# Mixture of experts on one core: row gathers issued during the second product, the second matrix's blocks taken in the order 0, 2, 1, 3, and the over-capacity path ahead of the last product

## The chip, the core and the metric

The kernel runs on one core of a Trainium2 chip. The core has TensorE (PE in the profile: matrix products; PEld is its weight load), VectorE (DVE), ScalarE (ACT), GpSimd (POOL) and SyncE (SP, which here issues the plain DMAs). GpSimd issues the DMAs that gather and scatter rows by an index. The metric is device microseconds of one execution; lower is better.

## The reference, cut to what matters

Attention over 4 x 576 tokens is followed by a dense block, and then by a mixture of 8 experts. The change lies in the experts alone. Each of the 2304 tokens goes to the one expert with the largest gate logit:

```
logits = x @ w_gate                      # x: 2304 x 512
e_idx = np.argmax(logits, axis=1)
...
for e in range(8):
    mask = e_idx == e
    h = np.maximum(x[mask] @ w1[e], 0.0)     # first product, 512 -> 1024
    ye = h @ w2[e]                           # second product, 1024 -> 512
    out[mask] = gate_w[mask, None] * eom[mask, e, None] * ye
```

## The kernel before

Everything is float32. Each product is made of three passes (`mm3`, `mm3n`): a matrix is split into a rounded part (`hi`) and the remainder (`lo`), and hi·hi, hi·lo and lo·hi are summed in PSUM. In `mm3n` the three passes are lines L425, L426 and L427; in `mm3` L419, L420 and L421. The third pass reads the `lo` part of the weights.

The token rows were written to a table `yd` in DRAM by the dense block. The experts are ranked by their token count and taken in an order `r` = 0 to 7 with fixed capacities `CAPS` = 352, 336, 320, 304, 288, 288, 272, 384, so three blocks of at most 128 rows for each. Per expert:

- `x_gather` (L732, POOL) fetches up to 128 rows per DMA into one of four `xr` buffers; `x_prep` transposes them on PE (L750) and splits them on ACT and DVE (L754).
- `ew_load` (SP, L763 for the first matrix, L766 for the second) brings a quarter of a weight matrix, "block" 0 to 3, 512 KB, into one of four `raw` buffers. It must wait until the split that used the buffer before is done.
- `ew_split` makes `hi` with a cast on ACT (L775) and `lo` with a subtraction (L777): blocks 0 and 2 on POOL, blocks 1 and 3 on DVE. The first matrix's tiles are `W0` to `W3` (hi) and `W4` to `W7` (lo), the second matrix's `W8` to `W11` (hi) and `W12` to `W15` (lo).
- `ga_pair` is a quarter of the first product: two of eight `h` tiles, f = 2i and 2i+1, from block i. ACT and DVE split each result (L803).
- `gb_step` is a quarter (`dc`) of the second product. It runs over f = 0 to 7 and takes block f // 2, so every `gb_step` needs all four blocks of the second matrix. ACT copies its result (L845).
- `o_step` transposes a block of results back (L861), DVE scales it into `orow` (L850) and POOL scatters it into the output (L851).

The instructions of the loop over `r` are issued on each engine exactly in the order of the code (`manual_schedule`), shown below with its main lines. A stage `r` has two halves: four `gb_step`s of expert r, with the first matrix and the rows of expert r+1 prepared in between, then four `ga_pair`s of expert r+1, with its second matrix prepared in between. `by_width` (L654) chooses by a branch on PE how many columns a product runs over. In stage 0, `overflow_tables` (L874) computes on DVE which experts have more tokens than their capacity.

The last expert's second product is `gb_rows`: three blocks of 24 products each, DVE's `orow`, and a scatter. `overflow` (L914) then reads one number into a register on every engine (L915) and branches (L916): if some expert is over its capacity, a loop does the surplus tokens in a general way. With these inputs none is, and the engines jump over the body. On the jump's arm each engine waits until its own earlier instructions have signalled, and adds to its semaphores what the skipped body would have added.

```
            for dc in range(KD):
                gb_step(r, dc)
                ...
                ew_split(r + 1, 0, dc)
                ew_load(r + 1, 1, dc)
            for i in range(4):
                ew_split(r + 1, 1, i)
                if i == 0 and r + 2 < E:
                    x_gather(r + 2)
                ga_pair(r + 1, 2 * i)
                if i < NBLK[r]:
                    o_step(r, i)
```

Of the kernel before, what the change touches and what calls it, by code (L numbers as in the profile page):

```python
# [22 lines left out]
NT, DM, DF, E = 2304, 512, 1024, 8  # L23
# [12 lines left out]
NBLK = [-(-c // P) for c in CAPS]  # L36
NBM = max(NBLK)
CMAX = max(CAPS)
CUTS = (0, 16, 48)
NEG = -1e30  # L40
OOB = 1.0e6
RING = 2 * G
# [7 lines left out]
def attention_moe_kernel(ctx: ExitStack, tc: tile.TileContext, q, k, vw_in, v4_in, w1, w2, w3, w_out,  # L50
# [32 lines left out]
    for j in range(4):  # L83
        nc.gpsimd.iota(ci[32 * j:32 * j + 32, 0:32], pattern=[[1, 32]], base=0, channel_multiplier=-1)
    nc.vector.tensor_copy(cj[:, 0:32], ci[:, 0:32])
    nc.vector.tensor_scalar(cj[:, 32:64], cj[:, 0:32], 0.0, NEG, op0=ALU.is_lt, op1=ALU.mult)
    nc.vector.tensor_scalar(cj[:, 64:96], cj[:, 0:32], 6.0, NEG, op0=ALU.is_gt, op1=ALU.mult)
    nc.vector.tensor_tensor(
        mask, cj[:, 32:64].unsqueeze(1).to_broadcast([P, 6, 32]),
        cj[:, 64:96].unsqueeze(1).to_broadcast([P, 6, 32]), op=ALU.add)  # L90
    nc.vector.memset(mask[0:32, 0, 0:3], NEG)
    nc.vector.memset(mask[96:128, 5, 27:32], NEG)
    eps4 = mt([P, 1], F32, "eps4")
# [551 lines left out]
    def by_width(r, C, products):  # L645
# [3 lines left out]
        def arm(a, b):  # L649
            if b - a == 1:  # L650
                products(C - CUTS[a])
                return
            m = (a + b) // 2
            with tc.If(rt["n"][r] > C - CUTS[m]) as cond:  # L654
                arm(a, m)
            with cond.Else():
                arm(m, b)

        arm(0, len(CUTS))

# [55 lines left out]
        pe[0] = next((i for i in reversed(nc.cur_bb.bb.instructions) if i.engine == mybir.EngineType.PE), None)  # L716
        return res

    def x_gather(r, half=None):
        C = CAPS[r]  # L720
        d = rt.setdefault("xr", {})
        for b in range(NBLK[r]):
            n = min(P, C - P * b)
            if (r, b) not in d:
                d[r, b] = bp.tile([P, DM], F32, name="xr", tag="xr", bufs=4)
            dst, src = d[r, b][0:n], yd
            if half == 0:
                dst, src = dst[:, 0:DM // 2], yd.rearrange("n (t d) -> (n t) d", t=2)
            elif half == 1:
                dst, src = dst[:, DM // 2:DM], yh  # L730
            idx = rt["g2"][0:n, b:b + 1] if half == 0 else rt["gi"][0:n, r, b:b + 1]
            ins = nc.gpsimd.indirect_dma_start(out=dst, out_offset=None, in_=src,  # L732
                                               in_offset=bass.IndirectOffsetOnAxis(ap=idx, axis=0))
        return ins
# [23 lines left out]
    def ew_load(r, m, i, t=None):  # L758
        reg = reg_of(r)
        if t is None:  # L760
            t = bp.tile([P, 1024], F32, name="raw", tag="raw", bufs=4)
        if m == 0:
            ins = nc.sync.dma_start(out=t,  # L763
                              in_=e_w1[bass.ds(reg, 1), P * i:P * i + P, :].rearrange("o p n -> p (o n)"))
        else:
            ins = nc.sync.dma_start(out=t,  # L766
                              in_=e_w2[bass.ds(reg, 1), P * i:P * i + P, :].rearrange("o p n -> p (o n)"))
        raws[r, m, i] = t
        return ins

    def ew_split(r, m, i):
        t = raws.pop((r, m, i))
        hi = w_tile(8 * m + i, [P, 1024])
        lo = w_tile(8 * m + 4 + i, [P, 1024])
        nc.scalar.copy(out=hi, in_=t)  # L775
        eng = nc.vector if i % 2 != (r == 0 and m == 1) or (r == 0 and m == 0) else nc.gpsimd
        ins = eng.tensor_tensor(lo, t, hi.bitcast(F32), op=ALU.subtract)  # L777
        ew[r, m, i] = (hi, lo)
        return ins
# [94 lines left out]
    def overflow_tables():  # L874
        cnt, rank = rt["cnt"], rt["rank"]
        s3 = [P, E, E]
        s4 = [P, E, NC]
        cap_t = bt([P, E], "cap_t")
        for r in range(E):
            nc.vector.memset(cap_t[:, r:r + 1], float(RANK_CAPS[r]))  # L880
        cm = bt(s3, "cm")
        nc.vector.tensor_tensor(cm, bc(rank, s3, 2), bc(i8, s3, 1), op=ALU.is_equal)
        nc.vector.tensor_tensor(cm, cm, bc(cap_t, s3, 1), op=ALU.mult)
        cap = bt([P, E], "cap")
        nc.vector.tensor_reduce(out=cap, in_=cm, axis=AX.X, op=ALU.add)
        ov = bt([P, E], "ov")
        nc.vector.tensor_tensor(ov, cnt, cap, op=ALU.is_gt)
        b0 = bt([P, NC], "b0")
        nc.vector.tensor_scalar(b0, i18, float(P), None, op0=ALU.mult)
        f1 = bt(s4, "f1")  # L890
        f2 = bt(s4, "f2")
        nc.vector.tensor_tensor(f1, bc(cnt, s4, 2), bc(b0, s4, 1), op=ALU.is_gt)
        nc.vector.tensor_scalar(b0, b0, float(P), None, op0=ALU.add)
        nc.vector.tensor_tensor(f2, bc(b0, s4, 1), bc(cap, s4, 2), op=ALU.is_gt)
        nc.vector.tensor_tensor(f1, f1, f2, op=ALU.mult)
        nc.vector.tensor_tensor(f1, f1, bc(ov, s4, 2), op=ALU.mult)
        fi = bt([P, E * NC], "fi", I32)
        nc.vector.tensor_copy(fi, f1.rearrange("p e b -> p (e b)"))
        an = bt([P, 1], "an")
        nc.vector.tensor_reduce(out=an, in_=ov, axis=AX.X, op=ALU.add)  # L900
        ai = bt([P, 1], "ai", I32)
        nc.vector.tensor_copy(ai, an)
        ee = bt([P, E, NC], "ee", I32)
        nc.vector.tensor_copy(ee, bc(i8, s4, 2))
        tt = tab[:, 0]
        gi = bt(s4, "ogi", I32)
        si = bt(s4, "osi", I32)
        nc.vector.tensor_scalar(gi, tt, -1.0, 0.0, op0=ALU.add, op1=ALU.max)
        nc.vector.tensor_scalar(f2, tt, 0.0, OOB, op0=ALU.is_equal, op1=ALU.mult)
        nc.vector.scalar_tensor_tensor(si.rearrange("p e b -> p (e b)"), tt.rearrange("p e b -> p (e b)"), -1.0,  # L910
                                       f2.rearrange("p e b -> p (e b)"), op0=ALU.add, op1=ALU.add)
        rt.update(fi=fi, ai=ai, ee=ee, ogi=gi, osi=si)
# [198 lines left out]
    et = mybir.EngineType  # L1111
    with tc.manual_schedule(engines={et.PE, et.DVE, et.Activation, et.Pool, et.SP}):
        for r in range(E - 1):
            for dc in range(KD):
                gb_step(r, dc)
                if dc < NBLK[r + 1]:
                    x_prep(r + 1, dc)
                ew_split(r + 1, 0, dc)
                ew_load(r + 1, 1, dc)
            for i in range(4):  # L1120
                ew_split(r + 1, 1, i)
                if i == 0 and r + 2 < E:
                    x_gather(r + 2)
                ga_pair(r + 1, 2 * i)
                if i < NBLK[r]:
                    o_step(r, i)
                if r + 2 < E:
                    ew_load(r + 2, 0, i)
                if (r, i) == (0, 1):
                    overflow_tables()  # L1130
        for b in range(NBLK[E - 1]):
            gb_rows(E - 1, b)
    overflow()
    bctx.close()


# [58 lines left out]
```

## Time and profile before

| what | value |
|---|---|
| median of 3 runs | 729.62 us (725.38 to 732.04) |
| the profiled execution's own time | 732.17 us |
| its span, first to last instruction | 730.1 us |
| mean granted TensorE clock | 0.983 |
| PE busy, share of the span | 95% |
| POOL, DVE, ACT busy | 46%, 52%, 39% |

The span is what the trace shows; 2.1 us of the execution's time lie outside it. PE's busy share counts overlapping instructions once. The experts' loop runs from about 500 us to 705 us of the span, `gb_rows` from there to 722 us, and the rest is the program's end. The windows in the rows below are microseconds from the span's start.

### The profile page before, as it was taken

The numbers are of one execution on the slowest core, as the hardware profiler recorded it, in microseconds if no ns is written. First come the engines' busy times: TensorE is split into PE (matmuls) and PEld (weight loads), VectorE is DVE, ScalarE is ACT, GpSimd is POOL, SyncE is SP. The second block draws the span as 40 slices with busy tenths as digits, with TensorE's granted clock in tenths as the row PEclk, the third lists the DMA queues.
The fourth block names the chain that finished last, engine by engine and source line by source line (L and its number), as shares of the span: only waits on it lengthen the run. The fifth ranks groups of instructions, "written<-read, shape, count | busy, mean of one in ns | idle before, by whom it ended". The sixth has DMA issues, their size and how long they took to land.

```text
span 730.1 us, 14874 instructions
## 1 busy us (share of the span) xinstructions
PE 690.3 (95%) x5710; PEld 659.1 (90%) x5711; DVE 381.6 (52%) x887; ACT 286.1 (39%) x664; POOL 332.4 (46%) x339
## 2 busy tenths in 40 slices
PE   5888999998999999999999999989999999989995
PEld 3787988898999999999999999969999999989994
DVE  8898889853645346253242342563545345345340
ACT  3455525562354136135212221234534545545520
POOL 5976468863474047124002020142636466567431
PEclk9999999998999999999999999989999999999999
DMA  8878545363143124111010100455647456566501
GB/s 325 266 252 275 199 137 193 108 196 119 50 136 110 44 73 119 64 41 45 23 44 1 43 1 30 146 194 173 211 127 235 127 191 216 176 208 231 170 31 42
DMA packets 38287, 98.08 MB, mean 134 GB/s; under 512 B 6019, under 2 KB 12931, under 8 KB 38193
## 3 DMA queue, kind: packets, MB, share of 16 engines
q1 hardware_dynamic: 34768, 86.82, 37.5%
q0 software_dynamic: 3424, 9.93, 3.7%
q8 instruction: 68, 1.11, 0.6%
q14 instruction: 27, 0.21, 0.1%
HBM read 84.93 MB, written 12.29 MB: 133 GB/s over the span
## 4 chain that ended last, share of the span: by engine, by line
PE 52%; issue 18%; POOL 16%; DMA 7%; DVE 6%; ACT 1%; SPq 0%; POOLq 0%; DVEq 0%; ACTq 0%
PE g L419 14%; PE g L421 13%; PE g L420 13%; POOL W L777 6%; POOL out_dram L851 3%; POOL xr L732 2%; DMA v<-in_v_dram 2%; PE at L282 2%; DMA vw<-in_vw_dram 1%; PE g L427 1%; PE at L222 1%; PE g L425 1%; DVE cv L140 1%; PE g L426 1%; PE at L278 1%
## 5 line engine op out<-in xcount | busy, mean ns | idle before, releaser
L419 PE MATMUL g<-xh,W 128*128 128x384 f32 x384 | 131.9, 343 | 0.9 <-ACT a L453 0.9
L421 PE MATMUL g<-xh,W 128*128 128x384 f32 x384 | 129.2, 337 | 0.8 <-POOL W L398 0.7
L420 PE MATMUL g<-xl,W 128*128 128x384 f32 x384 | 129.2, 336 | 0.0
L777 POOL TENSOR_TENSOR W<-raw,W 128x1024 fp32r<-128x1024 f32 x29 | 70.3, 2424 | 78.3 <-ACT W L775 78.3
L458 POOL TENSOR_TENSOR h<-a,h 128x384 fp32r<-128x384 f32 x30 | 30.6, 1020 | 101.6 <-ACT h L456 101.6
L419 PEld LDWEIGHTS g<-xh,W 128*128 128x128 f32 x384 | 72.2, 188 | 2.5 <-ACT a L453 1.2
L421 PEld LDWEIGHTS g<-xh,W 128*128 128x128 f32 x384 | 72.1, 188 | 1.9 <-POOL W L398 1.8
L420 PEld LDWEIGHTS g<-xl,W 128*128 128x128 f32 x384 | 72.2, 188 | 0.1
L427 PE MATMUL g<-h,W 128*128 128x320 f32 (+4 forms) x224 | 66.2, 296 | 3.9 <-POOL W L777 3.9
L425 PE MATMUL g<-h,W 128*128 128x320 f32 (+7 forms) x224 | 68.3, 305 | 1.2 <-ACT xT L754 0.8
L419 PE MATMUL g<-wc,h 128*128 128x272 f32 (+1 forms) x240 | 69.3, 290 | 0.0
L420 PE MATMUL g<-wc,h 128*128 128x272 f32 (+1 forms) x240 | 68.9, 289 | 0.0
L425 PE MATMUL g<-xT,W 128*128 128x288 f32 (+5 forms) x224 | 68.8, 307 | 0.0
L421 PE MATMUL g<-wc,h 128*128 128x272 f32 (+1 forms) x240 | 68.6, 288 | 0.0
L426 PE MATMUL g<-h,W 128*128 128x320 f32 (+4 forms) x224 | 66.1, 295 | 0.8 <-DVE h L803 0.8
L427 PE MATMUL g<-xT,W 128*128 128x320 f32 (+4 forms) x224 | 66.4, 296 | 0.0
L426 PE MATMUL g<-xT,W 128*128 128x320 f32 (+4 forms) x224 | 66.3, 296 | 0.0
L775 ACT CAST W<-raw 128x1024 fp32r<-128x1024 f32 x61 | 63.2, 1048 | 5.5 <-DMA raw<-in_moe_w_dram 5.5
L777 DVE TENSOR_TENSOR W<-raw,W 128x1024 fp32r<-128x1024 f32 x32 | 41.4, 1294 | 38.0 <-ACT W L775 33.2
L454 DVE TENSOR_TENSOR a<-g,a 128x384 f32<-128x384 f32 x48 | 26.6, 554 | 55.0 <-PE g L421 47.0
L803 DVE SCALAR_TENSOR_TENSOR h<-g,h 128x288 fp32r<-128x288 f32 (+6 forms) x64 | 30.5, 486 | 31.0 <-ACT h L803 20.2
L803 ACT ACTIVATE h<-g 128x288 fp32r<-128x288 f32 (+6 forms) x64 | 27.4, 436 | 48.6 <-PE g L427 37.4
(266 smaller groups left out, 1746.6 us busy)
## 6 DMA issues: line engine op xcount, KB each, us to landing
raw<-in_moe_w_dram SPq DMA_DIRECT2D x61, 512.0 KB
f64w<-in_moe_w_dram SPq DMA_DIRECT2D x16, 512.0 KB
f<-in_moe_w_dram SPq DMA_DIRECT2D x16, 512.0 KB
vw<-in_vw_dram SPq DMA_DIRECT2D x16, 384.0 KB
kc<-in_k_dram SPq DMA_DIRECT2D x16, 288.0 KB
qT<-in_q_dram SPq DMA_DIRECT2D x16, 288.0 KB
kz<-in_k_dram SPq DMA_DIRECT2D x32, 144.0 KB
v<-in_v_dram SPq DMA_DIRECT2D x16, 288.0 KB
```

What stands on the lines that cost most here:

```text
L419: nc.tensor.matmul(ps, whi, xhi, start=first, stop=False)
L420: nc.tensor.matmul(ps, whi, xlo, start=False, stop=False)
L421: return nc.tensor.matmul(ps, wlo, xhi, start=False, stop=last)
L425: nc.tensor.matmul(ps[:, 0:w], whi, xhi[:, 0:w], start=first, stop=False)
L426: nc.tensor.matmul(ps[:, 0:n], whi, xlo[:, 0:n], start=False, stop=False)
L427: nc.tensor.matmul(ps[:, 0:n], wlo, xhi[:, 0:n], start=False, stop=last)
L454: nc.vector.tensor_tensor(a, pp[1][:, 0:G], a, op=ALU.mult)
L458: eng.tensor_tensor(lo, a, hi.bitcast(F32), op=ALU.subtract)
L775: nc.scalar.copy(out=hi, in_=t)
L777: ins = eng.tensor_tensor(lo, t, hi.bitcast(F32), op=ALU.subtract)
L803: return nc.scalar.activation(out=t[:, 0, 0:C], in_=ps[:, 0:C], func=AF.Relu), nc.vector.scalar_tensor_tensor(t[:, 1, 0:C], ps[:, 0:C], 0. ...
L851: ins = nc.gpsimd.indirect_dma_start(out=out, out_offset=bass.IndirectOffsetOnAxis(ap=rt["si"][0:n, r, b:b + 1], axis=0), in_=t[0:n], in_o ...
```

## The change

A constant `W2ORDER` gives the order in which the second matrix's blocks are loaded and split: 0, 2, 1, 3. The three gathers for expert r+2, which stood together behind the first split in the `ga_pair` half, are spread one by one over the first three `gb_step`s. The call of `overflow` is moved ahead of the last expert's `gb_rows`.

```diff
+W2ORDER = (0, 2, 1, 3)
...
-    def x_gather(r, half=None):
+    def x_gather(r, half=None, blocks=None):
...
-        for b in range(NBLK[r]):
+        for b in range(NBLK[r]) if blocks is None else blocks:
...
                 ew_split(r + 1, 0, dc)
-                ew_load(r + 1, 1, dc)
+                if r + 2 < E and dc < NBLK[r + 2]:
+                    x_gather(r + 2, blocks=(dc,))
+                ew_load(r + 1, 1, W2ORDER[dc])
             for i in range(4):
-                ew_split(r + 1, 1, i)
-                if i == 0 and r + 2 < E:
-                    x_gather(r + 2)
+                ew_split(r + 1, 1, W2ORDER[i])
                 ga_pair(r + 1, 2 * i)
...
+    overflow()
+    with tc.manual_schedule(engines={et.PE, et.DVE, et.Activation, et.Pool, et.SP}):
         for b in range(NBLK[E - 1]):
             gb_rows(E - 1, b)
-    overflow()
```

The order of instructions that follows from it is shown at three places. Line numbers of the changed kernel are higher by one (from `x_gather` on). A UNCONDITIONAL_BRANCH row is an engine's step from one block of code to the next.

POOL in stage 3, from the split of the first matrix's block 2 (`W6`) to the last scatter of the stage, before:

```order
L777 TENSOR_TENSOR W6_8744<-raw_8392,W2_8743 128x1024
L654 UNCONDITIONAL_BRANCH
L777 TENSOR_TENSOR W12_8832<-raw_8569,W8_8831 128x1024
L732 DMA xr_8835<-yd_72,b_gi_5790 128x512
L732 DMA xr_8837<-yd_72,b_gi_5790 128x512
L732 DMA xr_8839<-yd_72,b_gi_5790 32x512
L654 UNCONDITIONAL_BRANCH
L851 DMA out_0_dram<-orow_8937,b_si_5791 2304x512
L654 UNCONDITIONAL_BRANCH
L851 DMA out_0_dram<-orow_9044,b_si_5791 2304x512
L777 TENSOR_TENSOR W14_9052<-raw_8747,W10_9051 128x1024
L851 DMA out_0_dram<-orow_9142,b_si_5791 2304x512
```

and after:

```order
L778 TENSOR_TENSOR W6_8748<-raw_8392,W2_8747 128x1024
L733 DMA xr_8751<-yd_72,b_gi_5790 32x512
L655 UNCONDITIONAL_BRANCH
L778 TENSOR_TENSOR W12_8838<-raw_8571,W8_8837 128x1024
L655 UNCONDITIONAL_BRANCH
L852 DMA out_0_dram<-orow_8937,b_si_5791 2304x512
L778 TENSOR_TENSOR W14_8954<-raw_8662,W10_8953 128x1024
L655 UNCONDITIONAL_BRANCH
L852 DMA out_0_dram<-orow_9044,b_si_5791 2304x512
L852 DMA out_0_dram<-orow_9142,b_si_5791 2304x512
```

Between the splits of the second matrix's blocks 0 (`W12`) and 2 (`W14`) three gathers and two scatters stood before; now it is one scatter. The other two gathers stand ahead of `W6`, behind the first matrix's block 0.

DVE in the `ga_pair` half of stage 5, before:

```order
L803 SCALAR_TENSOR_TENSOR h0_10436<-g1_10351,h0_10436 128x272
L803 SCALAR_TENSOR_TENSOR h1_10439<-g1_10352,h1_10439 128x272
L850 TENSOR_SCALAR orow_10447<-tr_10442,b_gv_6014 128x512
L654 UNCONDITIONAL_BRANCH
L777 TENSOR_TENSOR W13_10464<-raw_10168,W9_10463 128x1024
L803 SCALAR_TENSOR_TENSOR h2_10543<-g1_10467,h2_10543 128x272
L803 SCALAR_TENSOR_TENSOR h3_10546<-g1_10468,h3_10546 128x272
L850 TENSOR_SCALAR orow_10554<-tr_10549,b_gv_6014 128x512
```

and after:

```order
L804 SCALAR_TENSOR_TENSOR h0_10436<-g1_10351,h0_10436 128x272
L804 SCALAR_TENSOR_TENSOR h1_10439<-g1_10352,h1_10439 128x272
L851 TENSOR_SCALAR orow_10447<-tr_10442,b_gv_6014 128x512
L655 UNCONDITIONAL_BRANCH
L804 SCALAR_TENSOR_TENSOR h2_10543<-g1_10467,h2_10543 128x272
L804 SCALAR_TENSOR_TENSOR h3_10546<-g1_10468,h3_10546 128x272
L851 TENSOR_SCALAR orow_10554<-tr_10549,b_gv_6014 128x512
L655 UNCONDITIONAL_BRANCH
L778 TENSOR_TENSOR W13_10562<-raw_10263,W9_10561 128x1024
```

The split of block 1 (`W13`) moves behind the second pair's `h` tiles and the second `orow`. In stage 0 it moves in the same way behind `overflow_tables`, whose instructions stand directly behind that `orow`.

PE between the last `ga_pair` of expert 7 and the first product of `gb_rows`, before:

```order
L427 MATMUL g1_11398<-xT_6254,W7_11091 128x336
L654 UNCONDITIONAL_BRANCH
L419 MATMUL g2_11479<-W8_11096,h0_11185 128x512
L420 MATMUL g2_11479<-W12_11097,h0_11185 128x512
L421 MATMUL g2_11479<-W8_11096,h0_11185 128x512
```

and after:

```order
L428 MATMUL g1_11398<-xT_6254,W7_11091 128x336
L655 UNCONDITIONAL_BRANCH
L916 TENSOR_LOAD b_ai_6777
L917 COMPARE_AND_BRANCH
L921 COMPARE_AND_BRANCH
```

The register load L916 and the branch L917 now stand where `gb_rows` followed directly; they stood behind its last product before. L921 is the first row of the body that L917 jumps over; the first product of `gb_rows` stands behind that body.

## Rows read from the trace of the kernel before

**Rows 1.** The page, busy time of each engine over the whole span.

```profile
PE 690.3 (95%) x5710; PEld 659.1 (90%) x5711; DVE 381.6 (52%) x887; ACT 286.1 (39%) x664; POOL 332.4 (46%) x339
```

**Rows 2.** The waits of PE, 500 to 722: total us, times, longest.

```profile
PE g L427 <- POOL W L777: 3.9, 3, 1.3
PE g L426 <- DVE h L803: 0.8, 1, 0.8
PE g L425 <- ACT xT L754: 0.8, 1, 0.8
PE g L425 <- issue: 0.5, 1, 0.5
```

**Rows 3.** The timeline of PE: start, us, what [idle before].

```profile
534.42 0.41 PE L426 MATMUL g<-h,W 128*128 128x320 f32 x1 [0.83 <-DVE h L803]
...
623.04 0.38 PE L427 MATMUL g<-h,W 128*128 128x240 f32 x1 [1.29 <-POOL W L777]
623.26 0.28 PE L425 MATMUL g<-h,W 128*128 128x240 f32 x1
623.37 0.28 PE L426 MATMUL g<-h,W 128*128 128x240 f32 x1
...
704.71 0.33 PE L427 MATMUL g<-xT,W 128*128 128x368 f32 x1
704.88 0.40 PE L419 MATMUL g<-W,h 128*128 128x512 f32 x1
...
721.23 0.40 PE L421 MATMUL g<-W,h 128*128 128x512 f32 x1
```

**Rows 4.** The timeline of POOL.

```profile
526.53 2.44 POOL L777 TENSOR_TENSOR W<-raw,W 128x1024 fp32r<-128x1024 f32 x1
...
610.31 2.51 POOL L777 TENSOR_TENSOR W<-raw,W 128x1024 fp32r<-128x1024 f32 x1 [2.25 <-ACT W L775]
612.97 1.79 POOL L732 DMA_INDIRECT xr<-yd,b_gi  x1 [0.15 <-issue]
...
616.33 0.87 POOL L732 DMA_INDIRECT xr<-yd,b_gi  x1 [0.30 <-issue]
...
618.84 1.75 POOL L851 DMA_INDIRECT out_dram<-orow,b_si  x1 [0.30 <-DVE orow L850]
620.60 2.39 POOL L777 TENSOR_TENSOR W<-raw,W 128x1024 fp32r<-128x1024 f32 x1
...
722.70 0.98 POOL L851 DMA_INDIRECT out_dram<-orow,b_si  x1 [4.54 <-DVE orow L850]
```

**Rows 5.** The timeline of DVE.

```profile
525.98 3.03 DVE L893 TENSOR_SCALAR b_b<-b_b 128x18 f32<-128x18 f32 x1
529.04 0.31 DVE L894 TENSOR_TENSOR b_f<-b_b,b_cap 128x144 f32<-128x144 f32 x1
...
612.13 1.76 DVE L777 TENSOR_TENSOR W<-raw,W 128x1024 fp32r<-128x1024 f32 x1
...
618.50 1.21 DVE L777 TENSOR_TENSOR W<-raw,W 128x1024 fp32r<-128x1024 f32 x1
...
621.34 0.46 DVE L803 SCALAR_TENSOR_TENSOR h<-g,h 128x288 fp32r<-128x288 f32 x1 [0.35 <-ACT h L803]
```

**Rows 6.** The timeline of ACT in stage 3.

```profile
610.97 1.05 ACT L775 CAST W<-raw 128x1024 fp32r<-128x1024 f32 x1
```

**Rows 7.** Line L916, from 700: duration ns min/median/max, first and last start.

```profile
L916 PEldq EVENT_SEMAPHORE  x2: 51/51/51, 721.7 to 721.8; - x2
...
L916 PEldq COMPARE_BRANCH  x1: 342/342/342, 717.8 to 717.8; - x1
...
L916 POOLq INC_SWDGE_SEM  x1: 1214/1214/1214, 723.8 to 723.8; - x1
```

**Rows 8.** Line L1190, the program's end, from 722; columns as above.

```profile
L1190 POOLq DRAIN  x3: 46/107/4233, 725.1 to 729.9; - x3
```

**Rows 9.** Line L654, branches of PE, 648 to 658.

```profile
L654 PEldq COMPARE_BRANCH  x6: 208/208/2475, 649.4 to 656.5; - x6
```


## The prediction

> **What bounds the kernel now.** I read the page first: PE is busy for 95% of the span, no other engine for much over half of it [rows 1]. So what can be gained without fewer products lies where PE stands still, and at the program's two ends. The waits of PE in the experts' part say how much that is: 3.9 us in three waits of 1.3 us for POOL's L777, 0.8 us once for DVE's L803, 0.8 us and 0.5 us that the view puts down to ACT and to issue, 6.0 us together out of 222 us [rows 2]. Everything else that the change touches runs beside a busy PE.
>
> The timeline shows what the three waits are. At 623.04 us PE stands before an L427, the third pass of the first `gb_step` of stage 4, which reads the `lo` part of a weight block [rows 3]. POOL's last split of the half-stage before ran from 620.60 to 622.99 us and released it [rows 4]. POOL makes `lo` of blocks 0 and 2, block 0 ran at 610.31, so this is block 2. It came late although its cast must have been ready long before: between the two splits POOL issued three gathers, from 612.97 us to about 617.2 us, and two scatters, the second of which ended at 620.59 us [rows 4]. The other two waits are the same instruction with the same releaser, one and two stages later. The stages before them have more tokens per expert, so PE reaches the `gb_step` later and no wait shows there.
>
> **The wait for block 2 goes (-3.9 us).** After the change the second split in POOL's queue is that of block 2, and only one scatter stands ahead of it. In the stage shown, block 0's split ends at 612.82 us. The scatter behind it costs 1.0 us if it runs like the shorter DMAs and 1.8 us if it runs like the longer ones [rows 4]; so block 2's split starts between 614.0 and 614.8 us, with gaps of 0.2 us counted in, and ends 2.4 us later, at 616.4 to 617.2 us. The cast it needs is the one that ACT runs from 610.97 to 612.02 us, as the second of the half-stage [rows 6], so ACT doesn't hold it. PE wanted the block 1.29 us before 623.04, at 621.75 us. The reserve is 4.5 us or more. All three waits go: 3.9 us.
>
> What is late next in that `gb_step`? Block 1 is now split third, on DVE, behind the second `orow`. PE needs it after six passes of the `gb_step`, at 0.11 us each (the step from 623.26 to 623.37 us) [rows 3] some 0.7 us before it stopped, at about 621.0 us. DVE gets to it at about 615.4 us (the cast is done and the second `orow` through). Then the `h` tiles f = 6 and 7: the last one's `lo` is done at 621.80 us [rows 5]. PE would want it in the second pass of f = 7. The stop was before the third pass of f = 4; eight passes later, at 0.11 us, is 622.6 us. Reserve 0.8 us: this is the next limit, and it is not reached. DVE does the same work in the half-stage as before, only with block 1 later, and the split of block 3 (618.50 us) and the last two `h` tiles are behind it in both orders.
>
> Here the trace gives a warning that I priced. DVE's split at 612.13 us took 1.76 us, the one at 618.50 us 1.21 us [rows 5]; the first began while POOL's split still ran, until 612.82 us, and ended 1.07 us after it [rows 4]. Such splits of the two engines evidently follow each other. After the change block 1's split on DVE (from 615.4 us) meets block 2's on POOL (until 616.4 to 617.2 us), so it ends at about 617.5 to 618.3 us rather than 616.6 us. Then two `h` tiles (0.46 us each), an `orow` (about 0.7 us), block 3's split (1.2 us) and the last two `h` tiles bring the last one to 621.3 to 622.1 us, against 622.6 us wanted. The delay is used up by DVE's pauses and costs nothing, with 0.5 us left at the worse end.
>
> The Trainium skill (SBUF — State Buffer, section "SBUF: two separate sides") says that DVE and GpSimd share one pair of SBUF ports as an exclusive lock held for the whole instruction, which applies to a DVE operation with two SBUF inputs against a GpSimd operation that reads SBUF. The trace agrees with it in the rows named above, and it speaks against moving POOL's and DVE's splits onto each other, as this change does.
>
> **The wait in stage 0 goes too (-0.8 us).** PE's wait at 534.42 us is for a DVE `h` tile [rows 3]. DVE was late because `overflow_tables` held it: its L893, over 18 numbers a partition, took 3.03 us, and the next instruction started at 529.04 us, just behind the end of POOL's block 2 split (526.53 to 528.97 us) [rows 4, 5]; similar DVE instructions beside it take 0.3 us. After the change block 2's split stands one pair earlier, at about 522 to 524.5 us, and L893 runs at 526 us without it: 2.7 us less on DVE. Block 1's split (1.2 us) moves from ahead of the tables to behind them, where it lies on the way to the last `h` tiles, but its place ahead of them stood in a pause that DVE spent waiting for ACT. So the last tile comes 2.7 - 1.2 = 1.5 us earlier, more than the 0.83 us that PE waited. If the two still meet, the wait would be 0.83 + 1.2 = 2.0 us instead: ends -0.8 and +1.2, and I take -0.8, since POOL's queue has nothing but one scatter ahead of the split.
>
> **The gathers in their new place (0).** They cost POOL 0.9 to 1.8 us each [rows 4]. They now stand behind the first matrix's splits of blocks 0 and 2 in the `gb_step` half, where POOL waits for ACT's casts between splits; the third stands ahead of the second matrix's block 0, whose split had 2.25 us of idle time before it at 610.31 us [rows 4]. The row buffers that they fill were read one `gb_step` earlier, so they wait for nothing. If a long one pushes block 0's split by 0.2 us, nothing on PE sees it: block 0 is wanted 9 us later. Their data come a half-stage earlier. On SP the loads for the next first matrix wait for splits in the new order; the last two waited for POOL until 623 us and now go 3 to 5 us earlier.
>
> **The two small waits (0, at best -1.2 us).** The 0.8 us put down to ACT stands behind a branch of 2.48 us, one of six in its stretch with a median of 0.21 us [rows 2, 9]. I don't see that the change removes such a branch; both waits follow some 6 us after a wait for POOL, so they may go with it.
>
> **The branch in the middle (+0.6 us).** PE's queue runs ahead of its array: at the old place the branch was taken at 717.8 us, 3.4 us ahead of the last product, and took 0.34 us [rows 3, 7]. Then come two semaphore instructions, of which the first waits for PE's own last product. That product ran until 721.63 us and the semaphores until 721.87 us: 0.24 us [rows 3, 7]. At the new place this stands behind the L427 at 704.71 us, which ends at 705.04 us; semaphores until 705.28 us, then a weight load and the first product at about 705.45 us, where it started at 704.88 us before [rows 3]: 0.6 us. On ACT, DVE and POOL the same arm takes about 2 us and runs beside the first block of `gb_rows`, 5.5 us of products. Ends: 0.4 us (semaphores alone) and 2.5 us, if the branch takes as long as the longest of [rows 9] and its lead doesn't hide it. I take 0.6 us, since the lead at 717.8 us was 3.4 us.
>
> The Trainium skill (Runtime: NRT & Kernel Launch, section "Instruction fetch mechanics") says that a taken branch to a target outside the fetched window makes the engine wait for a fetch of the target. One branch of six in [rows 9] looks like it, the one at the old place does not; by that rule the term would be the 2.5 us of the upper end.
>
> **The program's end (-1.2 us).** Behind the last scatter (722.70 to 723.68 us) POOL now runs L916's INC_SWDGE_SEM, 1.21 us from 723.8 us, and only then, at 725.1 us, the drain of 4.23 us with which the program ends [rows 4, 7, 8]. After the change the first stands 18 us earlier. If the drain takes as long as it does and starts earlier, 1.2 us are gained; if it waits for something that hangs on the last scatter, nothing. I take 1.2 us, because no other row ends near the drain's end; both ends stay in the range.
>
> **Sum.** -3.9 - 0.8 + 0.6 - 1.2 = -5.3 us. The profiled execution took 732.17 us, so it would take 726.9 us; it lies 2.55 us above the median, and I take the difference over to the median: 729.62 - 5.3 = **724.3 us**, 0.7% less.
>
> **The rivals.**
> 1. The wait takes another form. With block 2 early, `gb_step` stops before the last `h` tile's `lo` or block 3 instead, 0.5 to 0.8 us behind where it stopped. For it: DVE's splits now lie behind POOL's. Against it: the pauses above. It would leave about 0.6 us of each 1.3 us: 726.4 us.
> 2. The branch on PE is not hidden and the drain doesn't move: -4.7 + 2.5 = -2.2 us, 727.4 us. For it the one long branch; against it the lead.
> 3. Slower: DVE, behind POOL's split in each half-stage, falls so far back that its last `h` tile holds every first `gb_step`, in the early stages as well. It has to lose 0.5 us more than my worse end before PE feels it at all, and it decides the sign when PE stands 1.0 us longer in each of six stages, 6 us against the 5.3 us. Were it 1.5 us, 729.6 - 5.3 + 9 = 733 us. Against it: DVE is busy for 12 us or less of a stage of 27 us.
> 4. The change doesn't do what it says: the gathers hold POOL as long in their new place and delay the first matrix's blocks. Then 729.6 us. The order of instructions and POOL's idle times speak against it.
>
> **How the numbers follow.** Forecast 0.70, rival 1 0.12, rival 2 0.10, rival 3 0.05, rival 4 0.03. The unknown terms give the forecast -6.5 us (both small waits gone as well) to -2 us; the three runs of before lie 6.7 us apart, so a median of three may be off by 2 to 3 us either way. From 720.0 to 729.5 us no more than 2 in 10 is left out. One per cent, 7.3 us, is about what a measurement of this kernel can tell from no change. Below 722.3 us lie the forecast's better half with a favourable median: 0.25. Above 736.9 us only rival 3: 0.04. Within, 0.71.
>
> **What would show it.** Right: in the waits of PE no row for POOL's L777 and none for DVE's L803 at stage 0; POOL's second split of the second matrix about 4 us ahead of where it was; L893 near 0.3 us; about 0.6 us between the last L427 and the first product of `gb_rows`; POOL's final drain directly behind the last scatter. Wrong: a wait of PE for an `h` tile or a weight block on DVE at the first `gb_step` of a stage, a long branch at L916, or a drain that ends as long after the last scatter as before.

## The result, and the profile after

Six executions took 718.06 to 723.54 us, median 720.48 us, against 729.25 us for six of the kernel before. The ratio is 0.9894 (95% interval 0.9862 to 0.9926), so 7.7 us less (5.4 to 10.1); the two medians lie 8.8 us apart. Forecast were 5.3 us less and 724.3 us; the change went the way that was forecast, and further. The median lies 0.5 us inside the lower end of the range, in the part below 722.3 us to which the prediction gave 0.25.

The profiled execution took 720.14 us, with a span of 718.4 us. Of the 11.7 us between the two spans, 4.2 us lie ahead of the first `gb_step`, where the two programs have the same instructions and the mean granted clock of the first 200 us was 1.00 here and 0.97 before; over all thirteen traces that `gb_step` starts anywhere between 494.2 and 502.1 us, so they are not counted to the change. From the first product of stage 0's first `gb_step` to the end the span is 231.4 us before and 223.8 us after: 7.6 us.

This is where they went. Each row is a stretch of PE between two of its products, from the timeline of PE (us); the columns on the right are three of the experiments below. Halves that are not listed differ by 0.1 us at most, but for the `ga_pair` half of stage 4 (12.31 before, 12.57 after, 12.31 in the other kernels of the table; the view of waits shows nothing there, and the 0.26 us are not explained).

| stretch | before | after | order only | gathers only | order and gathers |
|---|---|---|---|---|---|
| `gb_step`s of stage 1 | 16.67 | 15.53 | 18.19 | 16.56 | 15.58 |
| `gb_step`s of stage 4 | 13.85 | 12.29 | 12.83 | 12.55 | 12.29 |
| `gb_step`s of stage 5 | 14.85 | 12.28 | 14.24 | 12.84 | 12.28 |
| `gb_step`s of stage 6 | 14.27 | 12.08 | 14.15 | 12.08 | 12.08 |
| last `ga_pair`s, to `gb_rows` | 17.48 | 17.94 | 17.48 | 17.48 | 17.63 |
| last product to the end | 8.90 | 7.91 | 8.89 | 9.28 | 9.29 |
| first `gb_step` to last product | 222.51 | 215.93 | 222.40 | 217.02 | 215.28 |

The busy time of the engines in the page of after answers to [rows 1]; no engine's busy time changed by more than 6 us.

```profile
PE 684.6 (95%) x5710; PEld 653.6 (91%) x5711; DVE 376.4 (52%) x887; ACT 286.5 (40%) x664; POOL 334.3 (47%) x339
```

The waits of PE from 500 to 722 us in after, where [rows 2] had four lines and 6.0 us, are one line, and it is the moved branch:

```profile
PE g L420 <- PEq L917: 0.3, 1, 0.3
```

The timeline of after, at the places of [rows 3 to 5], POOL, DVE and PE apart (start, us, what, idle before):

```profile
605.11 2.50 POOL L778 TENSOR_TENSOR W<-raw,W 128x1024 fp32r<-128x1024 f32 x1 [1.24 <-ACT W L776]
607.77 1.02 POOL L852 DMA_INDIRECT out_dram<-orow,b_si  x1 [0.16 <-issue]
608.82 2.41 POOL L778 TENSOR_TENSOR W<-raw,W 128x1024 fp32r<-128x1024 f32 x1
...
711.95 0.99 POOL L852 DMA_INDIRECT out_dram<-orow,b_si  x1 [4.54 <-DVE orow L851]
...
522.13 0.18 DVE L894 TENSOR_SCALAR b_b<-b_b 128x18 f32<-128x18 f32 x1
...
609.08 0.46 DVE L804 SCALAR_TENSOR_TENSOR h<-g,h 128x288 fp32r<-128x288 f32 x1 [0.92 <-ACT h L804]
...
610.12 2.21 DVE L778 TENSOR_TENSOR W<-raw,W 128x1024 fp32r<-128x1024 f32 x1
...
615.44 0.46 DVE L804 SCALAR_TENSOR_TENSOR h<-g,h 128x288 fp32r<-128x288 f32 x1 [0.23 <-ACT h L804]
...
693.44 0.33 PE L428 MATMUL g<-xT,W 128*128 128x368 f32 x1
694.07 0.47 PE L420 MATMUL g<-W,h 128*128 128x512 f32 x1 [0.30 <-PEq L917]
...
710.49 0.40 PE L422 MATMUL g<-W,h 128*128 128x512 f32 x1
```

The first `gb_step` of stage 4 starts at 614.80 us here and started at 620.00 us before, 5.20 us apart. On that scale POOL's split of block 2 ends at 616.4 us (611.23 + 5.20), where it ended at 622.99 us: 6.6 us earlier. The over-capacity tables' instruction on 18 numbers (L893 before, L894 now) took 0.18 us instead of 3.03 us.

The program's last part in after, by its two lines (duration in ns, minimum/median/maximum, then first and last start); it answers to [rows 7, 8]:

```profile
L917 PEldq EVENT_SEMAPHORE  x2: 51/51/51, 693.8 to 694.0; - x2
...
L917 PEldq COMPARE_BRANCH  x1: 1127/1127/1127, 691.3 to 691.3; - x1
...
L917 POOLq INC_SWDGE_SEM  x1: 1144/1144/1144, 692.5 to 692.5; - x1
...
L1192 POOLq DRAIN  x3: 46/164/5465, 711.7 to 718.1; - x3
```

The branch on PE took 1.13 us and began 2.2 us ahead of the last L428; it was over before that product started. POOL's INC_SWDGE_SEM stands 19 us ahead of the last scatter. The drain is recorded from 711.7 us, ahead of that scatter, but it ends 4.24 us behind the scatter's end (712.94 to 717.18 us); before, it ended 4.27 us behind the INC_SWDGE_SEM.

### The profile page after: what moved, and what is told of

Read it like the earlier page. It is cut to its first block, busy times and chain, and to the rows that moved or that the text cites. A ratio compares the mean times of both kernels' runs of the same rounds, so it can differ in the third digit from the quotient of the medians.

```text
span 718.4 us, 14883 instructions
## 1 busy us (share of the span) xinstructions
PE 684.6 (95%) x5710; PEld 653.6 (91%) x5711; DVE 376.4 (52%) x887; ACT 286.5 (40%) x664; POOL 334.3 (47%) x339
## 3 DMA queue, kind: packets, MB, share of 16 engines
HBM read 84.93 MB, written 12.29 MB: 135 GB/s over the span
## 4 chain that ended last, share of the span: by engine, by line
PE 64%; DMA 10%; issue 5%; DVE 5%; POOL 4%; ACT 1%; POOLq 0%; SPq 0%; DVEq 0%
PE g L420 13%; PE g L421 13%; PE g L422 13%; DMA xr<-yd,b_gi 6%; PE g L426 6%; PE g L428 6%; PE g L427 6%; PE at L283 1%; PE tr L751 1%; DMA vw<-in_vw_dram 1%; DVE wf L142 1%; PE tr L862 1%; DVE cv L141 1%; DVE cv L140 1%; PE at L223 1%
## 5 line engine op out<-in xcount | busy, mean ns | idle before, releaser
L420 PE MATMUL g<-wc,h 128*128 128x272 f32 (+1 forms) x240 | 68.6, 287 | 0.0
L421 PE MATMUL g<-wc,h 128*128 128x272 f32 (+1 forms) x240 | 68.3, 286 | 0.0
L422 PE MATMUL g<-wc,h 128*128 128x272 f32 (+1 forms) x240 | 67.8, 285 | 0.0
L428 PE MATMUL g<-xT,W 128*128 128x320 f32 (+4 forms) x224 | 66.5, 297 | 0.0
L428 PE MATMUL g<-h,W 128*128 128x320 f32 (+4 forms) x224 | 66.0, 295 | 0.0
L852 POOL DMA_INDIRECT out_dram<-orow,b_si x24 | 33.2, 1385 | 38.0 <-DVE orow L851 35.8
```

The costliest lines, as they stand in the source:

```text
L420: nc.tensor.matmul(ps, whi, xhi, start=first, stop=False)
L421: nc.tensor.matmul(ps, whi, xlo, start=False, stop=False)
L422: return nc.tensor.matmul(ps, wlo, xhi, start=False, stop=last)
L428: nc.tensor.matmul(ps[:, 0:n], wlo, xhi[:, 0:n], start=False, stop=last)
L852: ins = nc.gpsimd.indirect_dma_start(out=out, out_offset=bass.IndirectOffsetOnAxis(ap=rt["si"][0:n, r, b:b + 1], axis=0), in_=t[0:n], in_o ...
```

## The experiments

All ratios are to the kernel before, run beside them, with 95% intervals.

**One part alone, and two together.** Three kernels hold one part of the change each, a fourth the order and the gathers.

```diff
# order only: gathers and overflow() as before
+W2ORDER = (0, 2, 1, 3)
# gathers only: order 0, 1, 2, 3
+                if r + 2 < E and dc < NBLK[r + 2]:
+                    x_gather(r + 2, blocks=(dc,))
# path only: overflow() ahead of gb_rows, loop as before
# order and gathers: overflow() behind gb_rows
```

Expected of the order alone:

> Only the second matrix's order 0, 2, 1, 3; gathers and over-capacity path as before. Measure: from the first product of the first gb_step of stage 0 to the last product of gb_rows, 222.5 us before and 215.9 us after. Theory A (each of the two halves, order and gathers, is enough for the waits on POOL): in stage 3 the gathers end at 617.2 us, one scatter ends by 618.5 us, block 2's split ends at about 621.1 us, where PE wanted it at 621.75 us, so the three waits for POOL go; the collision of L893 with POOL's split in stage 0 stays (split about 525.2 to 527.6 us), with PE's wait of about 0.8 us; 216 to 217.5 us in the loop, and 4 to 6 us less than before in the time. Rival B (the gathers are what holds POOL, the order alone saves one scatter): block 2 still comes late in stages 4 to 6, waits of 0.1 to 1 us each stay, 218 to 221 us in the loop, 1 to 3 us less than before.

Measured: 0.9994 (0.9973 to 1.0015), no gain; loop 222.40 us. Both theories fell. The waits for POOL did go, as A had it, but others took their place. The waits of PE from 495 to 722 us:

```profile
PE g L427 <- DVE h L804: 2.0, 4, 1.2
PE g L426 <- issue: 1.1, 1, 1.1
PE g L426 <- ACT xT L755: 1.1, 1, 1.1
PE g L428 <- DVE W L778: 0.9, 1, 0.9
```

The timeline of the same kernel shows why, POOL first, then DVE:

```profile
617.41 2.41 POOL L778 TENSOR_TENSOR W<-raw,W 128x1024 fp32r<-128x1024 f32 x1
...
521.83 3.17 DVE L883 TENSOR_TENSOR b_cm<-b_rank,i 128x64 f32<-128x64 f32 x1
...
614.10 1.22 DVE L778 TENSOR_TENSOR W<-raw,W 128x1024 fp32r<-128x1024 f32 x1
...
617.27 3.63 DVE L778 TENSOR_TENSOR W<-raw,W 128x1024 fp32r<-128x1024 f32 x1
620.83 0.81 DVE L804 SCALAR_TENSOR_TENSOR h<-g,h 128x288 fp32r<-128x288 f32 x2
```

With three gathers still ahead of it, POOL's block 2 split meets DVE's block 3 split, the last one of the half-stage. That one takes 3.63 us instead of 1.22 us (it ends 1.1 us behind POOL's), and the last two `h` tiles stand behind it. This is the first rival of the prediction, in a kernel that has only half of the change.

Expected of the gathers alone:

> Only the gathers moved into the gb_steps; order 0, 1, 2, 3 and over-capacity path as before. Theory A: block 2's split waits for two scatters, the second of which waits for DVE's second orow (615.4 us in stage 3), so it ends at 618.9 to 619.8 us, 2 to 3 us ahead of the 621.75 us wanted; the three waits for POOL go; in stage 0 block 2's split starts at about 525.7 us and still meets L893, so PE's wait for the h tile stays at about 0.8 us; 216 to 217.5 us in the loop, 4 to 6 us less than before. Rival B': the second scatter's wait for DVE keeps block 2 late, 0.5 us or more of each wait stays, 219 us or more in the loop.

Measured: 0.9917 (0.9889 to 0.9944), loop 217.02 us: theory A. What is left is in its waits of PE (first fence) and on DVE's timeline (second), beside POOL's split from 522.54 to 524.95 us: a tables' instruction that takes 0.17 us elsewhere.

```profile
PE g L427 <- DVE h L804: 0.8, 1, 0.8
PE g L426 <- PE tr L751: 0.3, 1, 0.3
```

```profile
522.07 2.91 DVE L888 TENSOR_TENSOR b_ov<-r_cnt,b_cap 128x8 f32<-128x8 f32 x1
```

Expected of the path alone:

> Only the over-capacity path ahead of the last product; expert loop as before, so this is also a second look at the loop of before. Theory A: between the last L427-type product of the loop and the first of gb_rows 0.63 us instead of 0.17 us (+0.46 us), from the last product to the end of the program 7.9 us instead of 8.9 us (-1.0 us): together 0.5 us less than before, not measurable. The three waits of 1.3 us and the one of stage 0 return at their places. Of the two small waits (0.8 us behind a branch of 2.48 us in stage 5, 0.5 us in stage 6): if they are consequences of the waits for POOL some 6 us ahead of them, they return in this trace; rival: if they are chance, they are elsewhere or absent. Rival C for the gain of the whole change: its part beyond the waits is here, and this alone gains 2 us or more.

Measured: 0.9997 (0.9967 to 1.0027). The last `ga_pair`s up to `gb_rows` take 17.94 us against 17.48 us, as in after, and the last product is followed by 7.52 us instead of 8.90 us: theory A. The path alone doesn't carry the gain (rival C). The waits of PE show the loop of before a second time, the small waits too, at the same places:

```profile
PE g L428 <- POOL W L778: 3.8, 3, 1.3
PE g L426 <- ACT xT L755: 1.3, 1, 1.3
PE g L427 <- DVE h L804: 0.8, 1, 0.8
PE g L426 <- issue: 0.4, 1, 0.4
PE g L420 <- PEq L917: 0.3, 1, 0.3
```

Expected of order and gathers together:

> Order and gathers moved, over-capacity path behind gb_rows as before. Theory A: the whole gain of the loop, 222.5 - 7.0 = 215.5 us from the first gb_step to the last product (0.46 us less than after), the program's end 8.9 us; the time within 1 us of after, 6.5 to 8 us below before. L893 short (0.2 to 0.4 us), no wait of PE for POOL or DVE in the loop. Rival C: 2 us or more above after, if the end of the program carried a part of the gain that the trace does not show.

Measured: 0.9925 (0.9903 to 0.9948), loop 215.28 us, and no wait of PE for anything in it: theory A in the loop. The time was 5.5 us below before (3.8 to 7.1), less than the 6.5 to 8 us expected, and the end took 9.29 us instead of the 8.9 us expected. The loop's whole gain of 7.2 us is here; the gathers alone have 5.5 us of it, the order adds 1.7 us to them and alone has 0.1 us. What it adds lies in stage 1 (1.0 us, the tables) and in small losses of stages 4 and 5 (0.3 and 0.6 us), not in the waits for POOL.

**DVE's reserve.** Block 1's split is done twice, or three times.

```diff
-                ew_split(r + 1, 1, W2ORDER[i])
+                ew_split(r + 1, 1, W2ORDER[i], 2 if W2ORDER[i] == 1 else 1)   # or 3
```

> The changed kernel with DVE's split of the second matrix's block 1 done twice (the same result), +1.2 us on DVE in each half-stage. By the trace of after, DVE's last h tile is done at 615.90 us in the first gb_step of stage 4 and PE wants it at about 617.2 us (start 614.80 us plus 22 passes of 0.11 us): reserve 1.2 to 1.4 us in stages 4 to 6, 0.5 us in stage 1, where the over-capacity tables stand ahead of it. Theory D (reserve as read there): only stage 1 waits, about 0.7 to 0.9 us longer; the loop takes 216.6 to 217 us instead of 215.9 us; the time within 1.5 us of after. Rival E (the reserve is the 0.5 us at the worse end of the prediction, or less): three more waits of 0.7 us and more, 218.5 us or more.

Measured: 0.9927 (0.9900 to 0.9955). One wait of 0.6 us in stage 1, none for DVE in stages 4 to 6, loop 217.09 us (theory D). The median lay 2.3 us above after's, where at most 1.5 us was expected; the two intervals overlap.

> The changed kernel with that split done three times, +2.4 us on DVE in each half-stage. Theory D: waits of PE for DVE's last h tile of about 1.0 us in the first gb_step of stages 4, 5 and 6 and of 1.9 us in stage 1. Theory F (the small waits are the price of a lost lead: PE's instruction queue stands with the wait, and the next fetch of instructions some 6 us later is not hidden): the small waits return, 0.5 to 1.3 us behind a long branch in stage 5 and 0.4 to 1.1 us inside stage 6, though POOL's block 2 is early; loop 222 to 224 us, time 6 to 8 us above after. Rival G (the small waits hang on where the gathers stand, since only kernels with the gathers in the old place showed them in stage 6): no small waits, loop 221 us at most.

Measured: 0.9988 (0.9963 to 1.0013); the gain is gone, loop 221.83 us. Its waits of PE for DVE from 494 to 717 us:

```profile
PE g L427 <- DVE h L805: 3.2, 4, 1.2
PE g L428 <- DVE W L779: 0.4, 1, 0.4
```

The waits for the last `h` tile are 0.65, 0.61 and 0.76 us in stages 4 to 6, less than the 1.0 us of theory D, and 1.2 us in stage 1, where 0.4 us for block 1's own split come on top. So DVE's reserve in the changed kernel lies between 1.2 us (no wait) and 1.8 us (2.4 less 0.6). A small wait came back in stage 5 (0.55 us), none in stage 6: neither F nor G as stated.

**The end of the program.**

```diff
-    overflow()                                  # left out in the first kernel
...
-        o_out(r, b, ps)                         # no scatter for the last block in the second
+        o_out(r, b, ps, b < NBLK[r] - 1)
```

> The changed kernel without the over-capacity path (the branch and its body are left out; the tables are still computed). Theory: the step on PE between the loop's last product and the first of gb_rows goes back from 0.63 us to 0.17 us (-0.46 us), the end of the program stays at 7.5 to 8.0 us behind the last product's start, since POOL's INC_SWDGE_SEM was out of it already; 0.5 us below after, not measurable. Rival: the place of the path costs more than the trace of after shows (2 us or more below after).

Measured: 0.9871 (0.9847 to 0.9895), median 719.02 us, 1.5 us below after; the step on PE is gone, 7.51 us behind the last product's start. The kernel differs by more than the path: six products of `gb_rows` stand between the last `ga_pair`s here. By the traces it is 1.2 us shorter than after from the first `gb_step` to the end: 0.46 us are the step, 0.40 us the end, 0.26 us the `ga_pair` half of stage 4. The 2 us of the rival are not there.

> The changed kernel without the scatter of the last 128 rows (they stay unwritten). Theory H (POOL's final drain runs 4.2 us from POOL's last own work): POOL's last work is then the scatter that ended at 707.4 us, the drain is over at about 711.7 us, and the end follows DVE's last orow: 2.4 to 3.5 us behind the start of the last product instead of 7.9 us, time 4.4 to 5.5 us below after. Rival I (the drain is a closing step of 4.2 us that starts when all engines are through): 6.5 to 7.5 us behind the last product, 0.5 to 1.4 us below after.

Measured: 0.9803 (0.9777 to 0.9829), median 715.00 us, 5.5 us below after; 2.65 us behind the last product. Theory H. POOL's last scatter in the timeline, and the drain in the view of the program's last line:

```profile
707.00 0.98 POOL L854 DMA_INDIRECT out_dram<-orow,b_si  x1 [4.53 <-DVE orow L851]
```

```profile
L1194 POOLq DRAIN  x3: 113/179/5373, 706.8 to 713.3; - x3
```

The drain again ends 4.2 us behind the scatter (707.98 to about 712.1 us), now 1.1 us behind the start of the last product.

**The two small waits.** In all kernels one branch of PE in stage 5, 4.6 us behind the stage's first product where nothing waits, is longer than its neighbours; in the kernel before it is the 2.48 us of [rows 9]. A table from the traces, with PE's fetch of instructions (a 16 KB transfer on the DMA queue of kind "instruction") that falls there:

| kernel | branch, us | fetch landed to branch's end | PE's extra time behind it |
|---|---|---|---|
| path only | 3.06 | 1.49 | 1.55 |
| order only | 2.84 | 1.49 | 1.34 |
| before | 2.48 | 1.50 | 0.98 |
| split three times | 2.05 | 1.50 | 0.55 |
| gathers only | 2.04 | 1.48 | 0.54 |
| split twice | 1.92 | 1.48 | 0.42 |
| order and gathers | 1.34 | 1.48 | 0 |
| after | 1.30 | 1.48 | 0 |

PE's extra time is the branch's length less 1.5 us, whether or not PE had waited for POOL or DVE a few us earlier (split twice and gathers only had no such wait in that stage). So the length decides, and it follows the landing of the fetch. (In gathers only a branch of stage 4 took 1.73 us, and PE lost 0.27 us there.) The fetch in turn came at the tail of a burst of weight loads. In before SP issued two of 512 KB at 649.20 and 649.77 us, just behind POOL's late split (646.77 to 649.17 us); their transfers filled the DMA engines from 650.2 to 653.3 us, and the fetch began at 652.43 us, 0.1 us behind the branch's start. In after the same loads were issued at 637.67 and 639.41 us, their transfers were over at 643.0 us, and the fetch began at 643.16 us, 1.1 us ahead of the branch. The small wait of stage 6 stands behind no long branch, but the pattern is the same: in before two loads were issued at 676.15 and 676.73 us, their transfers filled the DMA engines from 677.3 to 680.2 us, a fetch began at their tail and landed at 680.86 us, and PE went on at 682.27 us, 1.4 us later. No run tests that stage by itself.

The first trial left out those two loads of the kernel before:

> The kernel before, with the loads of the first matrix's blocks 2 and 3 left out for the experts of stages 6 and 7 (both blocks are split from block 1's buffer, so those experts' products are of other numbers; all other work stays). Question: what the small waits of PE in stages 5 and 6 hang on. Over the ten traces so far the long branch in stage 5 ended 1.5 us after a 16 KB fetch of instructions landed, PE's extra time was the branch's length less 1.5 us (0.98 of 2.48, 1.34 of 2.84, 0.42 of 1.92, 0 of 1.30), and the fetch began where a burst of weight loads ended. Before, that burst is these two blocks, whose loads SP issued at 649.20 and 649.77 us, just behind POOL's late split. Theory J (the fetch stands behind the loads): without them the branch lasts 1.5 us or less and the small waits of stages 5 and 6 go (1.0 and 0.6 us of the loop), while the three waits of 1.3 us for POOL stay: loop 220.9 us instead of 222.5 us. Rival F (PE's lost lead behind the waits for POOL): the branch may be shorter, but waits of 0.4 us or more stay in both stages; loop 222 us or more.

```diff
+        if r in (6, 7) and m == 0 and i > 1:
+            raws[r, m, i] = raws[r, m, 1]
+            return None
```

Measured: 1.0018 (0.9990 to 1.0046), branch 2.66 us, extra time 1.21 us. It doesn't decide: SP issued the next two loads of the same size in their place, at 646.13 and 646.71 us. The second trial kept the buffers held:

```diff
+        if r in (6, 7) and m == 0 and i > 1:
+            ins = nc.sync.dma_start(out=t[:, 0:8], in_=...)          # 4 KB, not 512 KB
...
+            ins = eng.tensor_tensor(lo[:, 0:8], own[:, 0:8], ...)    # holds the buffer
```

> The kernel before, with the loads of the first matrix's blocks 2 and 3 for experts 6 and 7 cut from 512 KB to 4 KB each (both blocks are split from block 1's buffer, plus a tiny split of the cut one that holds the buffer as long as before; those experts' products are of other numbers). In the run before this one other loads took the place of the two that were left out, so the burst stayed and so did the long branch (2.66 us) and the wait (1.2 us). Theory J (PE's fetch of instructions stands behind the burst of weight loads): with the burst gone the fetch starts 1 us or more earlier, the branch in stage 5 is 1.5 us or less, the small waits of stages 5 and 6 go (1.0 and 0.6 us), and the three waits of 1.3 us for POOL stay. Rival F (PE's lost lead behind the waits for POOL): small waits of 0.4 us or more stay in both stages.

Measured: 0.9995 (0.9961 to 1.0029). Its branches of PE from 648 to 658 us, and its waits of PE from 636 to 663 us:

```profile
L654 PEldq COMPARE_BRANCH  x6: 208/208/935, 650.5 to 656.6; - x6
```

```profile
PE g L427 <- POOL W L783: 1.3, 1, 1.3
```

The fetch began 4.72 us behind the stage's first product, where it began 6.27 us behind it in before. The branch is 0.94 us and the small wait is gone, while the wait for POOL stands ahead of it as before; stage 6 has none of "issue" either. Theory J in stage 5, and F falls there. (In stage 6 the cut loads also moved the splits, and PE waited there 0.8 us for an `h` tile of DVE instead of 1.3 us for POOL, so only stage 5 is a clean comparison.)

The opposite, loads held back in the changed kernel:

> The changed kernel, with the loads of the first matrix's blocks 2 and 3 for expert 6 held back until DVE's last h tile of the half-stage ahead of stage 5 is done (a one-column write into each buffer on DVE makes them wait); nothing else changes. In after these two loads were issued at 637.67 and 639.41 us and their burst ended 3.4 us behind the first product of stage 5; held back they start 2 to 2.5 us behind it and end at 5.3 to 5.8 us. Theory J: the fetch starts there, the branch ends 7.7 to 8.2 us behind the first product instead of 5.9 us, and PE waits 1.6 to 2.2 us behind it in stage 5, with no wait for POOL or DVE ahead of it. Rival F: no wait in stage 5. If the fetch is asked for before the burst begins, theory J expects no wait either, and the run tells nothing.

Measured: 0.9888 (0.9846 to 0.9931), no wait in stage 5. SP issued the held-back loads 1.4 and 2.0 us behind the stage's first product, and their transfers ran from 2.3 to 5.7 us. The fetch began at 3.0 us, 0.7 us behind the start of those transfers and in among them, landed within 0.9 us, and the branch took 0.83 us. So loads under way did not hold this fetch. It may have been asked for before they began, the case that the expectation sets aside, but the trace doesn't show when a fetch is asked for. That a burst of loads delayed the fetch of before is shown by the run with the cut loads, in one stage of one trace; when a burst does so stays open.

## Why the prediction was right, and where it was too small

- **The three waits for POOL: -3.9 us, right in cause.** The three halves lost 6.3 us (1.56, 2.57, 2.19). Each of the three waits cost 1.46 to 1.48 us of PE's pace, where the view of waits shows 1.29 to 1.32 us of idle time: 4.4 us. A small wait behind two of them is most of the rest (below). Either the order or the gathers alone takes these waits away.
- **What is late next:** DVE's last `h` tile, as named. The prediction had it done at 621.3 to 622.1 us with 0.5 to 1.3 us left. It was done at 621.1 us on the scale of before (615.90 + 5.20), and the doubled splits put the reserve at 1.2 to 1.8 us. Block 1's split was stretched by POOL's to 2.21 us and ended at 617.5 us on that scale, inside the forecast of 617.5 to 618.3 us; the pauses behind it took that up.
- **Most of what the text credited to the order belongs to the gathers.** It told the gain as block 2 standing second in POOL's queue. The order alone gave nothing, since waits for DVE took the place of those for POOL: it is the gathers' leaving that moves POOL's split from DVE's last split to an earlier one. The sum did not need the split between the two, so it stood.
- **Stage 0: -0.8 us, right; 1.1 us measured** in the `gb_step`s of stage 1. L893 ran without POOL's split, and a tables' instruction was held again (3.17, 2.91 us) in the kernels with the order or the gathers alone, where the split still met them. So this term needs both.
- **The small waits: 0, "at best -1.2 us". This is the mis-sized term.** Both went, 1.6 us (0.98 and 0.64 us of PE's pace). The prediction saw that SP's last two loads would go 3 to 5 us earlier (5.0 and 3.9 us at stage 5, counted from the stage's first product), and followed them no further; in before, PE's instruction fetch came at the tail of their transfers, and with the loads cut to 4 KB it came 1.55 us earlier and the wait was gone. Stage 6 shows the same pattern, without a test of its own.
- **The branch in the middle: +0.6 us; measured +0.46 us.** The branch itself took 1.13 us, three times as long as at the old place, and the lead covered it, as argued.
- **The end: -1.2 us; measured -1.0 us here.** Over six profiled kernels with the path ahead or left out it was 7.51 to 7.91 us (before 8.90 us, and 8.89 to 9.29 us in five others with the path behind). The drain follows POOL's last work, as taken: it ends 6.7 us behind the start of the last product in those six and 8.1 us behind it in the other six, 1.4 us apart. The step after the drain comes in two sizes, 0.8 and 1.2 us, which is not explained; before had the short one and after the long one.
- **The sum.** By the table the terms are 6.3 + 1.1 + 1.0 us gained and 0.5 + 0.3 us lost, 7.6 us against the 5.3 us forecast. That is more than the 6.5 us which the prediction took for the best end of its terms. The median lies inside the range because the range also allowed 2 to 3 us for the noise of a median; the cause was right, but that the number fell inside is in part luck.

Of the rivals, the first came true only with half of the change (its price should read 726.1 us: 724.3 us and three times 0.6 us), the second not at all (the branch was hidden, the drain moved). The third would need more than 1.2 us of DVE's time per half-stage on top of what the change has. The fourth falls too: after shows no wait of PE for a weight block or for rows.

## What to carry to other kernels

A late transfer or split is not done with its own wait: follow what it releases. Here POOL's late split let SP issue two 512 KB loads late, and PE's 16 KB of instructions came at their tail. Where DVE's and POOL's splits exclude each other, as here, moving one is a choice of which of the other's operations it meets; let it meet one with pauses behind it, not the last before a deadline. And here POOL's last work set the end of the program by its drain (5.5 us less without the last scatter), so whatever POOL can do earlier should not stand behind it.

## What the runs showed of the hardware

- A DVE operation with all its inputs in SBUF that began less than 0.7 us ahead of a POOL split, or during it, was held to about the end of POOL's, however small it was: 8 numbers a partition took 2.91 us, 18 took 3.03 us; a split of 1.22 us took 3.63 us and ended 1.1 us behind POOL's. One that began 0.8 us or more ahead was not held: the split at 609.31 us took 1.23 us beside POOL's from 610.31 us (before), and POOL's took 2.51 us there instead of 2.41 us. The Trainium skill (SBUF — State Buffer, section "SBUF: two separate sides") gives the pair of ports to whichever starts first. By the recorded starts DVE was first in these three as well (617.27 against 617.41 us, for one), so a recorded start that is 0.7 us earlier or less does not tell who holds the ports.

```profile
609.31 1.23 DVE L777 TENSOR_TENSOR W<-raw,W 128x1024 fp32r<-128x1024 f32 x1 [4.35 <-ACT W L775]
```

- DVE's `h` operations, which read one input from PSUM, kept their 0.46 us beside a POOL split (609.08 us beside 608.82 to 611.23 us in after).
- PE's branch in stage 5 ended 1.48 to 1.50 us after its fetch of instructions had landed, in all thirteen traces, and was 0.83 to 3.06 us long; only what exceeded 1.5 us was felt. The Trainium skill (Runtime: NRT & Kernel Launch, section "Instruction fetch mechanics") names the stall of a taken branch. What the runs add is that the fetch began 1.55 us earlier, counted from the stage's first product, when two 512 KB loads ahead of it were cut to 4 KB each; the held-back loads of the last run did not hold it.
